# Block-causal attention into a gated MLP: how the row maxima reach the score products, and how the row sums are totalled

## The chip, the cores and the metric

The kernel runs on one core of a Trainium2 chip. The metric is the device time of one execution in microseconds. Five engines work side by side, each through its own list of instructions in order: TensorE (PE in the profile; its weight loads are shown as PEld), VectorE (DVE), ScalarE (ACT), GpSimd (POOL) and SyncE (SP), which here only issues DMA transfers. An instruction that waits for another engine holds up everything behind it in its own engine's list.

## The reference

```python
scores = scale * np.matmul(q, k.transpose(0, 1, 3, 2))     # 8 batches, 8 heads, 576 x 64
mask = block_i >= block_j                                   # blocks of 64
scores = np.where(mask, scores, -1000000000.0)
scores = scores - np.max(scores, axis=-1, keepdims=True)
attn = np.exp(scores)
attn = attn / (np.sum(attn, axis=-1, keepdims=True) + 1e-09)
x = np.matmul(attn, v)                                      # then heads side by side: 4608 x 512
a = x @ w1; b = x @ w2                                      # 512 x 1024 each
h = a * b @ w3                                              # 1024 x 1024
return h @ w_out                                            # 1024 x 512
```

## The kernel before, in words

The work goes by pairs of heads: 32 pairs (eight batches of four), and the two heads of a pair are `j = 0` and `j = 1`. For each head TensorE makes transposed scores (keys on the partitions, queries along the row) in tiles of 128 keys, `s_tile` (L255), ScalarE takes their exponential, and TensorE multiplies by the values (`pv`, L312). Numbers are kept as sums of a high and a low piece, so a product of two full numbers is two or three matmuls.

**The maxima.** A softmax row needs its maximum. `shift_mask` (L174) makes the scores once more, in 16 bits, as the products `mx` (L192, six tiles, up to 512 wide), VectorE reduces each to a column of the tile `m` (L196), TensorE turns the nine columns into nine rows (`mt`, L200), ScalarE copies these with a minus sign (`ms`, L202), and `shift` (L207) sends them by DMA into rows of the operand tiles `qk0` and `qk1` (L218): nine rows of 64 numbers for each head, laid out along one partition. There they stand as one more row of the contraction, so that the score product itself subtracts the maximum. For a pair `n` that is done while pair `n - 1` is at work. Up to pair 4 these transfers go on ScalarE's queue, from pair 5 on on SP's (`queue`, L168). The same queue of SP carries the load of the raw q, k and v of a pair (`load`, L101, 896 KB, two buffers), the copies of q and k to the other half of the partitions (L232, L233) and the outputs (L447).

**The second copy of the operands.** `prep_qk` (L220) casts q and k of a head into `qk0` or `qk1` on VectorE (L166), copies by DMA, and GpSimd makes the low piece (L235). `prep_v` (L238) casts the values on ScalarE and GpSimd makes their low piece `vs` (L248). The load of pair `n + 2` overwrites the buffer of pair `n`, so it waits for the last reader of that buffer, which is L248 for `j = 1`. That step in turn runs only when the value product of the pair ahead has let go of `vs`.

**The row sums.** `sums` (L330) reduces the sums over the keys to `part` on VectorE, `total` (L335) adds across partitions with one fp32 matmul of 36 columns against a 0/1 matrix (`groups4`, part of the tile `ident`), and `norm` takes the reciprocal and multiplies.

**The order.** TensorE's order is written out: for each pair and head a row of letters in `PLAN` (L46) is read from left to right. S is the next score tile or part of one, V and U the next value product, M the next step of `shift_mask` for the next pair, A and B steps of `prep_qk`, F the next piece of the MLP (six or so matmuls), R `sums`, N takes the values, Q prepares values and loads, T is `total` and the division. The MLP of a batch runs as F steps while the next batch's attention is at work; `DELAY` lets the first few F steps of pair 4 pass, which sets how far the MLP runs behind. The first four pairs have their own plan and share TensorE with the preparation of the weights. The other engines' lists are made by a scheduler from the program, so an instruction can stand there earlier or later than in the source.

## Time and profile before

| what | value |
|---|---|
| median of 3 timed runs | 971.45 us (969.41 to 972.49) |
| the profiled execution's own time | 970.15 us |
| span of its instructions | 968.3 us |
| PE busy | 938.8 us (97%) |
| DVE / ACT / POOL busy | 692.3 / 556.6 / 617.5 us |
| chain that ended last | PE 89% of the span |
| mean granted clock of TensorE | 0.996 |

In a row of a timeline stand the start in us from the span's start, the length in us, the engine, the line of the kernel, the operation, what it writes and reads, its shape and how many instructions were merged; in brackets the idle time ahead of it and who ended it. On SP a row is the issue of a transfer, not the transfer. Matmuls are pipelined, so their cost is read from start to start: one of 288 columns takes 0.13 us of TensorE, although each row says 0.29.

### The profile page before, as it was taken

The page shows a single profiled execution, that of the slowest core. Times are in us where ns is not written, and L with a number is a line of the kernel's source. Part 1 is how long each engine was busy: PE and PEld are TensorE (multiplying, and loading weights), DVE is VectorE, ACT ScalarE, POOL GpSimd, SP SyncE. Part 2 cuts the span into 40 slices and gives each one's busy share as a digit, 9 for nine tenths or more (in the row PEclk, how much of TensorE's full clock was granted, in tenths as well). Part 3 has the DMA queues.
Part 4 walks back from the last instruction along what each step waited for, and adds up shares of the span by engine and source line. Part 5 has one row for each costly group of instructions (what it writes and reads, how often), then busy time and mean ns, then how long its engine had stood idle before and what let it go on. Part 6 is the DMA issues. An engine that isn't in the chain of part 4 may idle for free.

```text
span 968.3 us, 18335 instructions
## 1 busy us (share of the span) xinstructions
PE 938.8 (97%) x6624; PEld 878.7 (91%) x6624; DVE 692.3 (72%) x1230; ACT 556.6 (57%) x1451; POOL 617.5 (64%) x605
## 2 busy tenths in 40 slices
PE   3898899999999999999999999999999999999998
PEld 1454469999999999999999999999999999999998
DVE  6787767788777777787787777777887777774100
ACT  7768736556565556565656555565555656553221
POOL 6766737677766767677776767676777667672211
PEclk9899999999999999999999999999999999999999
DMA  8976512212212221321222222222122122100000
GB/s 303 305 230 204 158 51 64 86 32 72 76 58 82 65 88 52 88 65 47 66 76 64 71 81 64 78 61 88 33 69 75 58 82 64 50 13 26 7 20 26
DMA packets 31303, 79.81 MB, mean 82 GB/s; under 512 B 5356, under 2 KB 13676, under 8 KB 31212
## 3 DMA queue, kind: packets, MB, share of 16 engines
q1 hardware_dynamic: 29788, 76.26, 25.7%
q10 hardware_dynamic: 1424, 2.38, 1.0%
q8 instruction: 52, 0.85, 0.4%
q14 instruction: 39, 0.32, 0.1%
HBM read 50.76 MB, written 9.44 MB: 62 GB/s over the span
## 4 chain that ended last, share of the span: by engine, by line
PE 89%; ACT 3%; DVE 3%; POOL 2%; issue 1%; DMA 1%; ACTq 0%; SPq 0%; DVEq 0%; POOLq 0%
PE ab L426 42%; PE o L442 21%; PE s L265 9%; PE x L320 9%; PE mx L192 4%; PE w L407 2%; POOL wbits L152 1%; ACT wbits L151 1%; ACT wy L150 1%; PE x L304 1%; DVE m L196 1%; ACT pe L273 1%; DMA qk<-ms 1%; DVE w L153 0%; PE tot L337 0%
## 5 line engine op out<-in xcount | busy, mean ns | idle before, releaser
L286 POOL TENSOR_TENSOR rsum<-rsum,p 128x448 f32<-128x448 f32 x224 | 185.8, 829 | 86.8 <-ACT p L280 78.3
L283 DVE TENSOR_TENSOR pl<-p,ph 128x448 fp32r<-128x448 f32 x168 | 149.4, 903 | 59.9 <-ACT ph L281 59.0
L435 POOL TENSOR_TENSOR gl<-g,gh 128x288 fp32r<-128x288 f32 x128 | 114.4, 894 | 121.9 <-ACT gh L434 121.9
L265 PE MATMUL s<-qk 128*128 128x288 f32 (+4 forms) x768 | 155.2, 311 | 6.1 <-ACT pe L273 3.6
L235 POOL TENSOR_TENSOR qk<-raw,qk 64x1152 fp32r<-64x1152 f32 x58 | 155.0, 2673 | 8.6 <-issue 5.6
L426 PE MATMUL ab<-xh,w2h 128*128 128x288 f32 x512 | 153.8, 300 | 0.0
L442 PE MATMUL o<-gh,wh 128*128 128x288 f32 x512 | 153.6, 300 | 0.0
L426 PE MATMUL ab<-xh,w1h 128*128 128x288 f32 x512 | 151.1, 295 | 0.0
L426 PE MATMUL ab<-xl,w2h 128*128 128x288 f32 x512 | 151.0, 295 | 0.0
L426 PE MATMUL ab<-xl,w1h 128*128 128x288 f32 x512 | 151.0, 295 | 0.0
L426 PE MATMUL ab<-xh,w1l 128*128 128x288 f32 x512 | 150.9, 295 | 0.0
L426 PE MATMUL ab<-xh,w2l 128*128 128x288 f32 x512 | 150.9, 295 | 0.0
L442 PE MATMUL o<-gh,wl 128*128 128x288 f32 x512 | 150.9, 295 | 0.0
L442 PE MATMUL o<-gl,wh 128*128 128x288 f32 x512 | 150.8, 295 | 0.0
L434 ACT CAST gh<-g 128x288 fp32r<-128x288 f32 x128 | 55.4, 433 | 143.1 <-DVE g L433 143.0
L265 PEld LDWEIGHTS s<-qk 128*128 128x128 f32 (+1 forms) x768 | 116.0, 182 | 17.9 <-ACT pe L273 9.4
L281 ACT ACTIVATE ph<-s 128x288 fp32r<-128x288 f32 x336 | 131.5, 393 | 0.0
L196 DVE TENSOR_REDUCE m<-mx 128x1 f32<-128x64 f32 (+3 forms) x320 | 128.4, 447 | 2.2 <-PE mx L192 0.2
L280 ACT ACTIVATE p<-s 128x448 f32<-128x448 f32 x224 | 85.4, 381 | 51.2 <-PE s L265 50.4
L283 DVE TENSOR_TENSOR pl<-rsum,ph 128x288 fp32r<-128x288 f32 x112 | 75.6, 676 | 49.6 <-ACT ph L281 45.6
L320 PE MATMUL x<-ph,vs 128*128 128x128 f32 x336 | 110.4, 329 | 0.0
L433 DVE TENSOR_TENSOR g<-ab,a 128x288 f32<-128x288 f32 x128 | 56.6, 442 | 69.8 <-PE ab L426 69.0
(76 smaller groups left out, 2180.4 us busy)
## 6 DMA issues: line engine op xcount, KB each, us to landing
raw<-in_qkv SPq DMA_DIRECT2D x31, 896.0 KB
qk<-qk SPq DMA_DIRECT2D x108, 144.0 KB
out_t<-o SPq DMA_DIRECT2D x64, 144.0 KB
wraw<-in_w3t SPq DMA_DIRECT2D x16, 512.0 KB
wraw<-in_w SPq DMA_DIRECT2D x16, 512.0 KB
wraw<-in_wout SPq DMA_DIRECT2D x8, 512.0 KB
qk<-qk ACTq DMA_DIRECT2D x16, 144.0 KB
qk<-ms SPq DMA_DIRECT2D x54, 2.2 KB
```

What stands on the lines that cost most here:

```text
L196: nc.vector.reduce_max(m[:, col : col + 1], sc, axis=AX.X)
L235: (nc.gpsimd if "late" in tl or n * j else nc.vector).tensor_tensor(out=qk[j][o, 2:4], in0=rqk[o], in1=qk[j][o, 0:2], op=ALU.subtract)
L265: nc.tensor.matmul(t[ks, at : at + q1 - q0], qk[j][:, k, kr], qk[j][:, q, q0:q1], start=(s == 0), stop=(s == 1))
L280: nc.scalar.activation(p32, t[ks, at : at + w], AF.Exp, scale=SCALE)
L281: nc.scalar.activation(ph[ks, o : o + w], t[ks, at : at + w], AF.Exp, scale=SCALE)
L283: nc.vector.tensor_tensor(out=low, in0=p32, in1=ph[ks, o : o + w], op=ALU.subtract)
L286: nc.gpsimd.tensor_tensor(out=r, in0=r, in1=p32, op=ALU.add)
L320: nc.tensor.matmul(xps[:, to : to + w], v[:, c, :], pr[:, a : a + w], start=(u < 2 and s == 0), stop=(u in (0, len(PV) - 1) and s == len(p ...
L426: nc.tensor.matmul(t[:, 0:HALF], l[:, c, fs], r, start=(c == 0 and s == 0), stop=(c == NC - 1 and s == 2))
L433: nc.vector.tensor_tensor(out=g32, in0=acc[1][:, 0:HALF], in1=a32, op=ALU.mult)
L435: nc.gpsimd.tensor_tensor(out=gl[:, f, :], in0=g32, in1=gh[:, f, :], op=ALU.subtract)
L442: nc.tensor.matmul(t[:, 0:HALF], l[:, f, es], r[:, f, :], start=(f == 0 and s == 0), stop=(f == NF - 1 and s == 2))
```

## The change

Five edits:

1. For every pair but the first, the maxima are no longer turned by TensorE and copied by ScalarE. VectorE turns the whole tile `m` (128 x 32) in blocks of 32 x 32 into `mr`. `m` is now one tile, cleared once. A head's nine rows of 64 then stand as two times nine rows of 32, so `shift` sends two transfers for each head where it sent one. The minus sign moves into the constants.
2. The last score tile of a head ends in two narrow products (64 keys by 64 queries). A step boundary is put between them, and the plan sets maximum products behind each of the two. The last of the maximum tiles of a pair comes later, behind the value products, and the reduction's end and the first `shift` come directly after it.
3. In the plan for `j = 1` one F stands between R and T now; in exchange one less follows T.
4. `total` splits the sums into three 16-bit pieces by four small VectorE instructions and adds three 16-bit matmuls of 36 columns; the 0/1 matrix is kept in 16 bits as well (`groups`).
5. `DELAY` is 4 where it was 3.

```diff
 PLAN = (
-    "B F B F S F S B F F S S F F F S M S M U M V F V V F V F R V M Q N",
-    "A S S A F F F S F M S F F F S S M A U M V V V F V F F V N Q F R T M F F",
+    "B F B F S F S B F F S S F F F S M S M S M U V F V V F V F R V M Q N",
+    "A S S A F F F S F S F F F S S M S M A U V V V F V F F V M M N Q F R F T F",
 )
-DELAY = 3
+DELAY = 4
...
+    m = cpool.tile([P, 32], F32, name="m")
+    nc.gpsimd.memset(m, 0.0)
...
         nc.vector.tensor_tensor(out=m[:, 8:9], in0=m[:, 8:9], in1=m[:, 9:10], op=ALU.max)
+        if n:
+            mr = work.tile([P, 32], F32, tag="mr", name=f"mr{n}")
+            nc.vector.transpose(mr, m)
+            ms_of[n] = mr
+            shift(n, 0)
+            yield
+            return
...
-        row = qk[j][x : x + 1, 0, :].rearrange("p (i r) -> p i r", r=BLK)
-        queue(n).dma_start(out=row.bitcast(F32), in_=ms_of[n][:, j * BLK : (j + 1) * BLK].bitcast(F32))
+        row = qk[j][x : x + 1, 0, :].rearrange("p (i h r) -> p i h r", h=2, r=32)
+        for h in range(2):
+            at = j * BLK + h * 32
+            queue(n).dma_start(out=row[:, :, h, :].bitcast(F32), in_=ms_of[n][at : at + NB, :])
...
             for s, (k, q) in enumerate(((1, 2), (3, 0))):
+                if s and c == 4 and n >= EARLY:
+                    yield
...
     def total(n, part, rr):
-        nc.tensor.matmul(tot[:, 0 : S // 16], groups4, part, start=True, stop=True)
+        parts = work.tile([P, 3, S // 16], BF16, tag="parts", name=f"parts{n}")
+        part = part.rearrange("p j b -> p (j b)")
+        for i in range(2):
+            nc.vector.tensor_copy(parts[:, i, :], part)
+            rest = part if i == 0 else parts[:, 2, :]
+            nc.vector.tensor_tensor(out=rest, in0=part, in1=parts[:, i, :], op=ALU.subtract)
+        for i in range(3):
+            nc.tensor.matmul(tot[:, 0 : S // 16], tl["groups"], parts[:, i, :], start=(i == 0), stop=(i == 2))
...
-    consts[0:NB, 1] = 1.0
+    consts[0:NB, 1] = -1.0
```

On SP's queue, at the end of pair 17, where the maxima of pair 18 (`ms18`) are sent and the load of pair 20 (`raw20`) is issued, this stood before:

```order
173 L218 DMA qk0_86<-ms18_6303 1x9x64
174 L447 DMA out_t<-o32_6312 128x288
175 L218 DMA qk1_87<-ms18_6303 1x9x64
176 L105 DMA raw20_6648<-in_qkv 128x1792
177 L447 DMA out_t<-o32_6354 128x288
```

And this stands there now (`mr18` are the turned maxima of pair 18):

```order
173 L106 DMA raw20_6729<-in_qkv 128x1792
174 L229 DMA qk0_86<-mr18_6341 1x9x32 x2
175 L467 DMA out_t<-o32_6394 128x288
176 L229 DMA qk1_87<-mr18_6341 1x9x32 x2
177 L467 DMA out_t<-o32_6444 128x288
```

The load of 896 KB has moved from behind the maxima to ahead of them. The same holds at the end of every pair from 4 to 28. The load itself still waits for the GpSimd step on `vs` (L248 before, L259 now) of pair 18.

On VectorE, at the end of pair 19, between the last score differences (`pl`, `ph`) and the value sum `x32`, this stood before:

```order
641 L166 CAST qk1_87<-raw20_6648 64x1152
642 L283 TENSOR_TENSOR pl_1112<-p19_1_6962,ph_1110 128x192
643 L283 TENSOR_TENSOR ph_1110<-p19_1_6967,ph_1110 64x64
644 L196 TENSOR_REDUCE m20_6819<-mx20_4_6972 128x1 x2
645 L196 TENSOR_REDUCE m20_6819<-mx20_5_6980 128x1 x2
646 L333 TENSOR_REDUCE part19_6701<-rsum_1111 128x18
647 L198 TENSOR_TENSOR m20_6819<-m20_6819 128x1
648 L352 TENSOR_TENSOR x32_19_6699<-x19_1_6873,xlow19_1_7016 64x576
```

And now (`parts19` are the three 16-bit pieces):

```order
729 L296 TENSOR_TENSOR ph_1108<-p19_1_7049,ph_1108 64x64
730 L198 TENSOR_REDUCE m_91<-mx20_4_7054 128x1 x2
731 L346 TENSOR_REDUCE part19_6782<-rsum_1109 128x18
732 L170 CAST qk1_87<-raw20_6729 64x1152
733 L353 CAST parts19_7124<-part19_6782 128x36
734 L355 TENSOR_TENSOR part19_6782<-part19_6782,parts19_7124 128x36
735 L353 CAST parts19_7124<-part19_6782 128x36
736 L355 TENSOR_TENSOR parts19_7124<-part19_6782,parts19_7124 128x36
737 L198 TENSOR_REDUCE m_91<-mx20_5_7093 128x1 x2
738 L200 TENSOR_TENSOR m_91<-m_91 128x1
739 L372 TENSOR_TENSOR x32_19_6780<-x19_1_6949,xlow19_1_7103 64x576
740 L203 STREAM_TRANSPOSE mr20_7099<-m_91 128x32
```

The cast of `qk1` for the next pair has moved from ahead of the last score differences to behind the row sums, the last maximum is taken behind the four small instructions, and the turn of the maxima stands behind the value sum.

More of the change, by code (lines that the diff above doesn't have):

```diff
@@ L129, in open_late @@
         tl["late"] = pool
+        tl["groups"] = pool.tile([P, P], BF16, name="groups")
+        nc.gpsimd.tensor_copy(tl["groups"], groups4)
         tl["ph"] = pool.tile([P, PW], F32R, name="ph")
@@ L181, in shift_mask @@
         yield
-        m = work.tile([P, 32], F32, tag="m", name=f"m{n}")
         groups = [((7, 0, 512),), ((8, 0, 512),), ((0, 0, 64), (6, 0, 448)), ((1, 0, 128), (5, 0, 384)),
@@ L201, in shift_mask @@
         ms = work.tile([64, P], F32R, tag="ms", name=f"ms{n}")[32 : 32 + NB]
-        nc.scalar.mul(out=ms, in_=mt[0:NB, 0:P], mul=-1.0)
+        nc.scalar.copy(ms, mt[0:NB, 0:P])
         ms_of[n] = ms
```

## The prediction

> **What bounds the kernel now.** I read the page first, then TensorE's waits, then the timelines of all queues around one pair's end, since every edit lies there.
>
> ```profile
> span 968.3 us, 18335 instructions
> PE 938.8 (97%) x6624; PEld 878.7 (91%) x6624; DVE 692.3 (72%) x1230; ACT 556.6 (57%) x1451; POOL 617.5 (64%) x605
> ```
>
> ```profile
> PE mx L192 <- ACT qd L166: 12.2, 3, 5.9
> PE s L265 <- DMA qk<-ms: 1.5, 2, 1.0
> ```
>
> TensorE sets the time. It has waited for the maxima's transfers 1.5 us in all, twice, so these transfers land in time for nearly every pair. The question is what each edit takes off TensorE's list, and whether anything now reaches it late. The end of pair 15 on TensorE (start, length, what):
>
> ```profile
> 454.42 0.19 PE L320 MATMUL x<-ph,vs 128*128 128x64 f32 x1
> ...
> 455.18 0.29 PE L442 MATMUL o<-gl,wh 128*128 128x288 f32 x1
> 455.31 0.30 PE L337 MATMUL tot<-part,ident 128*128 128x36 f32 x2
> 455.45 0.28 PE L200 MATMUL mt<-ident,m 128*9 128x128 f32 x1
> 455.48 0.38 PE L442 MATMUL o<-gh,wh 128*128 128x288 f32 x1
> 455.70 0.29 PE L442 MATMUL o<-gh,wl 128*128 128x288 f32 x1
> ...
> 458.75 0.43 PE L265 MATMUL s<-qk 128*128 128x288 f32 x2
> ```
>
> I call the start of the next pair's score products E: 458.75 here. SP's queue ahead of it:
>
> ```profile
> 456.08 0.78 SPq L218 DMA_DIRECT2D qk<-ms  x1
> 456.98 0.37 SPq L447 DMA_DIRECT2D out_t<-o  x1
> 457.45 0.78 SPq L218 DMA_DIRECT2D qk<-ms  x1
> 458.33 0.40 SPq L105 DMA_DIRECT2D raw<-in_qkv  x1
> ```
>
> The first head's maxima are issued 2.67 us ahead of E, the load only at E - 0.42. At the end of the next pair, where TensorE works on the MLP's first half instead of its second (the pairs alternate so), it is tighter:
>
> ```profile
> 483.39 1.63 SPq L218 DMA_DIRECT2D qk<-ms  x2
> 485.12 0.40 SPq L105 DMA_DIRECT2D raw<-in_qkv  x1
> ```
>
> ```profile
> 485.60 0.42 PE L265 MATMUL s<-qk 128*128 128x288 f32 x2
> ```
>
> Issue to use is 2.2 us here, with no wait recorded: a lone transfer of maxima needs at most 2.3 us.
>
> **The change part by part.**
>
> *The total and the turn.* From 455.31 to 455.70 TensorE spends 0.39 us on the total (two records), the turn and one product of 288 columns, which alone costs 0.13: so 0.26 us for the first two. For 16-bit products as narrow the nearest rows are the maximum products behind the last value product:
>
> ```profile
> 442.53 0.19 PE L320 MATMUL x<-ph,vs 128*128 128x64 f32 x1
> 442.56 0.39 PE L192 MATMUL mx<-kb,qd 128*128 128x64 bf16 x2
> 442.63 0.85 PE L265 MATMUL s<-qk 128*128 128x288 f32 x4
> ```
>
> They follow each other 0.03 us apart. Three of them, the last followed by a full-precision product at 0.11, make 0.17 instead of 0.26: -0.09 us a pair. At worst each takes 0.11, which is +0.07. For 27 pairs: -2.4 us, bounds -5 and +2.
>
> *Maximum products behind narrow ones.* The same products stand in other places; a narrow product gains or loses by what follows it (0.03 ahead of a 16-bit product, as above). Some gain, some lose; I take 0, bounds of 0.1 us a pair either way, 3 us.
>
> *The four small instructions.* The nearest rows for 128 x 36 are
>
> ```profile
> L339 DVE TENSOR_SCALAR rr<-tot 64x18 f32<-64x18 f32 x56 | 9.8, 175 | 1.0
> L355 DVE RECIPROCAL rr<-rr 128x18 f32<-128x18 f32 x32 | 8.4, 262 | 0.6
> ```
>
> so 0.2 us each, 0.8 together. The total's products now stand some 2.6 us ahead of E, one F (six products, 0.8 us) later than before; the pieces are ready about E - 3.7 by the chain below. No wait, with 1.1 us to spare; that F is the cover, and without it 0.3 would be left. `DELAY` gives the division back the step that the move took: nothing.
>
> *What reaches SP's queue, and when.* Here is the cost. The load now stands ahead of the maxima, and waits for GpSimd's step on `vs`. That step stands on GpSimd behind the low piece of `qk1`, which needs VectorE's cast of `qk1`, and that cast now stands behind the row sums. VectorE before:
>
> ```profile
> 448.62 0.74 DVE L196 TENSOR_REDUCE m<-mx 128x1 f32<-128x128 f32 x2
> ...
> 450.34 0.76 DVE L166 CAST qk<-raw 64x1152 fp32r<-64x1152 f32 x1 [0.57 <-PE s L265]
> ...
> 452.07 1.22 DVE L196 TENSOR_REDUCE m<-mx 128x1 f32<-128x192 f32 x4
> 453.20 0.77 DVE L333 TRANSPOSE_TENSOR_REDUCE part<-rsum 128x18 f32<-128x576 f32 x1
> ...
> 455.31 0.76 DVE L352 TENSOR_TENSOR x<-x,xlow 64x576 f32<-64x576 f32 x1 [0.59 <-ACT xlow L351]
> ```
>
> Before, the sums end at 453.97. Now the cast (0.76) and two of the four reductions (some 0.5) no longer stand ahead of them, the two of 448.62 (0.74) do, so they end near 453.45, E - 5.3. The cast follows, to E - 4.55. GpSimd before, at the two ends:
>
> ```profile
> 452.03 2.67 POOL L235 TENSOR_TENSOR qk<-raw,qk 64x1152 fp32r<-64x1152 f32 x1
> 455.89 0.88 POOL L248 TENSOR_TENSOR vs<-raw,vs 128x320 fp32r<-128x320 f32 x1 [1.19 <-ACT vs L166]
> ```
>
> ```profile
> 481.78 0.80 POOL L435 TENSOR_TENSOR gl<-g,gh 128x288 fp32r<-128x288 f32 x1 [0.23 <-ACT gh L434]
> 483.15 0.88 POOL L248 TENSOR_TENSOR vs<-raw,vs 128x320 fp32r<-128x320 f32 x1 [0.57 <-ACT vs L166]
> ```
>
> From E - 4.55: 2.67 for the low piece, to E - 1.9; at every other end 0.80 for `gl`, to E - 1.05; 0.88 for `vs`: E - 0.95 or E - 0.15. (Before it was E - 1.98 and E - 1.57.) SP waits there, and behind it on its queue wait both heads' maxima and the outputs. So the load is issued at E - 0.9 or E - 0.1. The maxima are by then turned: pieces to E - 3.75, two reductions 0.6, the maximum 0.3, the value sum 0.76, the turn 0.2 (bounds 0.18 and 0.78, by L339 and by the turn of 576 columns): E - 1.85, at the other ends some 0.5 later.
>
> Then the wire. Engines' busy shares by microsecond after the load issued at 458.33 (the last two columns are the DMA engines' share and GB/s):
>
> ```profile
> 460.00:461.00 1.00, 1.00 (x9) 1.00 (x8) 0.81 (x1) 0.95 (x3) 0.49 (x1) 1.00 0.83 337
> 461.00:462.00 1.00, 1.00 (x9) 0.99 (x8) 0.46 (x1) 0.20 (x2) 0.00 (x0) 1.00 1.01 395
> 462.00:463.00 1.00, 1.00 (x9) 0.99 (x8) 0.00 (x0) 1.00 (x3) 0.11 (x1) 1.00 0.59 218
> 463.00:464.00 1.00, 1.00 (x10) 1.00 (x9) 0.72 (x1) 0.91 (x3) 1.00 (x1) 1.00 0.00 0
> ```
>
> All sixteen engines carry it until about 4.3 us after its issue. The only row with maxima sent next to a load is from the early pairs, on ScalarE's queue, in the chain that ended last:
>
> ```profile
> 98.19 5.22 DMA qk<-ms
> ```
>
> 5.22 us instead of 2.3. So I let the maxima land when the load has passed: 4.3 us and, an estimate, 0.3 for the end of the transfer, or 4.6 after the load's issue: E + 3.7 and E + 4.5. The Trainium skill's "DMA: Bandwidth & Descriptors" (Queues, rings and completion order) says that on each DMA engine the descriptors of one issuing queue are taken in ring order; no run here shows a small transfer behind a load on SP's own queue. The score tile's first product needs no maxima, the second does. TensorE stands for 3.65 us at 12 ends and 4.4 us at 13 (pairs 4 to 28): 43.8 + 57.2 = 101.0 us. If VectorE had nothing else in the way, the sums could end 0.7 us earlier, which leaves 3.0 as the low bound, 75 us; 4.7 is the high one, 118. At the last two ends there is no load, and the second of two issues (0.78 apart) is late by itself: E - 1.85 + 0.8 + 2 is some 0.9 each, 1.9 together.
>
> *The clock.* A standstill of this length has a second price:
>
> ```profile
> 42.30:45.70 3.40, 1.41 (x4) 0.34 (x2) 2.85 (x3) 3.38 (x7) 2.64 (x5) 1.00 0.91 343
> 45.70:49.10 3.40, 3.32 (x8) 2.34 (x9) 2.39 (x4) 3.31 (x7) 2.16 (x2) 0.51 0.68 204
> ```
>
> ```profile
> 45.78 0.61 PE L192 MATMUL mx<-kb,qd 128*128 128x512 bf16 x1 [2.07 <-ACT qd L166]
> ```
>
> After 2.07 us of idle TensorE the granted clock (third figure from the end) was 0.51 for the next 3.4 us. At half the clock 3.4 us of work lose 1.7; part of the slow stretch falls into the standstill, so I take 1.2 at each of 25 ends: 30 us, bounds 0 and 43.
>
> *The first pairs.* Their maxima go on ScalarE's queue: eight issues more (0.78 each, by the row at 456.08), and ScalarE now waits for VectorE's turn where it made the rows itself; a step over TensorE is saved. I take +2, bounds -2 and +8.
>
> Sum on the profiled execution (970.15 us): -2.4 + 101.0 + 1.9 + 30 + 2 = +132.5, or 1102.7. The median of the timed runs is 1.3 above that execution: 1104.
>
> **The rivals.**
>
> A. The standstill comes, but the clock falls only after a whole window of 3.4 us (the length of the slow row) without work. A standstill of 3.65 or 4.4 us holds a whole window in (3.65 - 3.4) / 3.4 = 7% or (4.4 - 3.4) / 3.4 = 29% of cases: some 5 ends of 25, 6 us instead of 30, and 1080 in all. Against it: 2.07 us did it once. It is the rule of the Trainium skill's "TensorE: Matmul & The Clock Gate" (HAM oscillation): one idle window of some 3.4 us, and the rate is halved. Chance 0.27.
>
> B. The maxima are not held up by the load, and land 2.3 us after their own issue. Behind the load's issue (0.40) the second of two, 0.78 later, lands at E + 2.4 or E + 3.2, so 12 x 2.4 + 13 x 3.2 = 70 us, and 20 us for the clock: 1063. Against it stands the row of 5.22 us. Chance 0.13.
>
> C. The load gets away much earlier than by my chain, and only the maxima's own lateness is left: 0.75 to 1.1 us at 27 ends, 25 us, no clock: 996. It needs GpSimd's step on `vs` by E - 5.5, when the values it overwrites are still in use. Chance 0.05.
>
> D. Faster or no change: VectorE turns the maxima so early that both transfers land ahead of E, and the load waits behind or is away. It decides from the turn's end: at E - 3.1 or earlier nothing is late, and the 2.4 us of TensorE stay: 969. VectorE's list speaks against it, since the last maximum product alone ends near E - 4.1, with 1.9 us of work behind it. Chance 0.05.
>
> **How the numbers follow.** My forecast has 0.50, at 1104 us; its own range by the bounds is 1080 to 1130. About 0.3% (3 us) is what a measurement of this kernel can tell from no change. A, B and C are slower by more; D lies at the edge, 0.02 faster and 0.03 the same. Slower: 0.50 + 0.27 + 0.13 + 0.05 = 0.95. For 8 in 10 the range takes in my case, A with a shorter standstill, and part of B: 1045 to 1130; C and D are left out.
>
> **What would show it.** Right: in the waits TensorE's `s` products wait for the transfer of `mr` some 25 times, 3.5 to 4.5 us each, and on SP the load's row stands ahead of the maxima's, issued less than 1 us before E; the granted clock falls below 1 throughout the stages of attention; the total's products don't wait. Wrong: a load issued well ahead of E - 2 breaks the VectorE and GpSimd chain; maxima that land 2.3 us after a load's issue break the wire's part; a full clock breaks the 30 us. If TensorE never waits for the maxima, the whole cost is wrong.

## The result, and the profile after

The changed kernel takes 1165.26 us in the median (1162.33 to 1166.76, 6 runs); the kernel before took 971.09 (968.45 to 972.93, 6 runs) beside it. The ratio is 1.1998, with a 95% interval of 1.1973 to 1.2024: 194 us slower. The direction was forecast, the size was not: 1165 lies above the range of 1045 to 1130.

The head of the page of the changed kernel:

```profile
span 1160.5 us, 18675 instructions
PE 1000.5 (86%) x6621; PEld 913.5 (79%) x6621; DVE 824.0 (71%) x1373; ACT 548.5 (47%) x1420; POOL 611.8 (53%) x607
```

TensorE is no longer busy throughout: 160 us of the span are idle, where 29.5 were. VectorE is busy 132 us longer, far more than its new instructions should take: at the forecast 0.8 us for the pieces and 0.2 for the turn, 27 pairs make 27 us. What TensorE waits for (total us, times, longest):

```profile
PE ab L446 <- DVE g L453: 51.6, 28, 3.1
PE s L278 <- DMA qk<-mr: 47.2, 25, 3.3
PE tot L357 <- DVE parts L353: 22.1, 13, 1.8
```

The second row is the one that was forecast, at half its size. The first and the third were not forecast: products of the MLP's first half wait until VectorE has emptied their buffer by making `g`, and the total waits for its pieces. The rest is the clock:

```profile
core 0: 1160.5 us, clock 0.954
```

A clock of 0.954 costs 0.046 x 1160.5 = 53 us, where 0.996 cost 4. (That takes the slow time for work, which it nearly all is: behind 150 us TensorE stood idle in 3 of the 92 us of slow stretches.) So the 192 us of span are, roughly: mr 45.7 more than before, g 51.6, pieces 22.1, clock 49; the other 23 are smaller waits, the first pairs (3.6: pair 4 starts at 139.81, not 136.24) and what is left, which the waits don't show.

**Where VectorE's time went.** Its groups by shape (busy us, mean ns of one), of the changed kernel, and one group of the kernel before:

```profile
L355 DVE TENSOR_TENSOR part<-part,parts 128x36 f32<-128x36 f32 x28 | 67.5, 2412 | 1.0
L355 DVE TENSOR_TENSOR parts<-part,parts 128x36 bf16<-128x36 f32 x28 | 5.5, 196 | 1.0
L200 DVE TENSOR_TENSOR m<-m 128x1 f32<-128x1 f32 x32 | 5.8, 181 | 0.0
```

```profile
L198 DVE TENSOR_TENSOR m<-m 128x1 f32<-128x1 f32 x32 | 19.1, 595 | 0.0
```

Two subtractions of the same size, one behind the other, take 2412 and 196 ns. The timeline of VectorE and that of GpSimd, at the end of pair 15, say why:

```profile
537.68 0.76 DVE L170 CAST qk<-raw 64x1152 fp32r<-64x1152 f32 x1
538.47 0.18 DVE L353 CAST parts<-part 128x36 bf16<-128x36 f32 x1
538.69 2.61 DVE L355 TENSOR_TENSOR part<-part,parts 128x36 f32<-128x36 f32 x1
541.33 0.88 DVE L353 CAST parts<-part 128x36 bf16<-128x36 f32 x1
542.25 0.20 DVE L355 TENSOR_TENSOR parts<-part,parts 128x36 bf16<-128x36 f32 x1
...
543.80 0.21 DVE L203 STREAM_TRANSPOSE mr<-m 128x32 f32<-128x32 f32 x1
```

```profile
538.58 2.66 POOL L246 TENSOR_TENSOR qk<-raw,qk 64x1152 fp32r<-64x1152 f32 x1 [2.49 <-DVE qk L170]
541.32 0.86 POOL L259 TENSOR_TENSOR vs<-raw,vs 128x320 fp32r<-128x320 f32 x1
```

The cast of `qk1` ends at 538.44, GpSimd starts its low piece at 538.58, and the subtraction that VectorE starts at 538.69 ends at 541.30, 0.06 us behind GpSimd's instruction. The next cast ends 0.03 us behind GpSimd's next one. So a small instruction of VectorE stands for as long as GpSimd's lasts; in what follows I call that a hold. It was there to be seen before the change, on the maximum of one column (L198, 595 ns in the mean above, 181 ns now):

```profile
453.90 0.82 DVE L198 TENSOR_TENSOR m<-m 128x1 f32<-128x1 f32 x1
```

It ended at 454.72, and the low piece of the row quoted in the prediction (452.03, 2.67 us) at 454.70. There it cost nothing that the waits show.

TensorE at the same end, and at the end of the next pair, where it works on the MLP's first half:

```profile
542.26 0.41 PE L357 MATMUL tot<-parts,groups 128*128 128x36 bf16 x2 [1.75 <-DVE parts L353]
546.97 0.37 PE L278 MATMUL s<-qk 128*128 128x288 f32 x1 [1.69 <-DMA qk<-mr]
```

```profile
574.42 0.40 PE L446 MATMUL ab<-xh,w2h 128*128 128x288 f32 x1 [3.07 <-DVE g L453]
582.10 0.58 PE L278 MATMUL s<-qk 128*128 128x288 f32 x1 [2.41 <-DMA qk<-mr]
```

SP ahead of the first of these two, the load and then both transfers of the first head's maxima:

```profile
542.20 0.35 SPq L106 DMA_DIRECT2D raw<-in_qkv  x1
544.04 1.59 SPq L229 DMA_DIRECT2D qk<-mr  x2
```

In VectorE's list `g` stands behind the held subtraction, so TensorE waits 3.07 us for it. I call the stretch from a pair's last score product to E its tail. The forecast's chain can be laid beside the trace. These are times in us from the end of a pair's last score product, at the ends where TensorE works on the second half of the MLP (median over pairs 6 to 29, from starts and ends in the trace; the forecast's, given from E, with E at 8.45):

| | before | forecast | after | e1 | e20 | e14 |
|---|---|---|---|---|---|---|
| cast of qk1 ends | 0.79 | 3.90 | 3.90 | 3.90 | 0.79 | 0.79 |
| GpSimd's low piece ends | 4.39 | 6.55 | 6.70 | 6.72 | 4.41 | 4.39 |
| pieces ready | - | 4.70 | 7.90 | - | 5.13 | 5.18 |
| total starts on TensorE | 5.04 | 5.85 | 5.78 | 5.83 | 6.01 | 5.82 |
| vs done, load may go | 6.46 | 7.50 | 7.63 | 7.68 | 6.60 | 6.46 |
| maxima turned | - | 6.60 | 9.47 | 7.77 | 6.69 | 4.66 |
| E | 8.45 | 8.45 | 11.01 | 8.42 | 8.57 | 8.38 |

The columns e1, e20 and e14 are experiments below. At these ends the cast, the low piece and the load came within 0.15 us of the forecast, the pieces 3.2 us later, and the maxima were turned 2.9 us later. At the other ends, with the MLP's first half, the chain of the load did not hold: the cast comes at 4.55, the low piece at 7.31, and `vs` is done only at 10.73, where the forecast had 8.30. GpSimd makes a `gl` between the two (574.97, at the end of pair 16), and that waits for the `g` behind the held subtraction.

### The profile page after: what moved, and what is told of

It is laid out like the page before. It is cut to its first block, busy times and chain, and to the rows that moved or that the text cites. A ratio compares the mean times of both kernels' runs of the same rounds, so it can differ in the third digit from the quotient of the medians.

```text
span 1160.5 us, 18675 instructions
## 1 busy us (share of the span) xinstructions
PE 1000.5 (86%) x6621; PEld 913.5 (79%) x6621; DVE 824.0 (71%) x1373; ACT 548.5 (47%) x1420; POOL 611.8 (53%) x607
## 4 chain that ended last, share of the span: by engine, by line
PE 47%; DVE 28%; issue 9%; DMA 8%; ACT 6%; POOL 1%; SPq 0%; ACTq 0%; DVEq 0%; POOLq 0%
PE ab L446 24%; PE o L462 7%; DMA qk<-mr 6%; PE s L278 6%; DVE part L355 6%; PE w L427 3%; DVE m L198 3%; DVE pl L296 3%; PE x L333 3%; DVE x L372 2%; DVE qk L170 2%; PE mx L194 2%; DVE part L346 2%; DVE parts L353 2%; DVE g L453 2%
## 5 line engine op out<-in xcount | busy, mean ns | idle before, releaser
L296 DVE TENSOR_TENSOR pl<-p,ph 128x448 fp32r<-128x448 f32 x168 | 168.3, 1028 | 96.8 <-ACT ph L294 96.8
L455 POOL TENSOR_TENSOR gl<-g,gh 128x288 fp32r<-128x288 f32 x128 | 103.2, 806 | 220.8 <-ACT gh L454 220.8
L278 PE MATMUL s<-qk 128*128 128x288 f32 (+4 forms) x768 | 172.0, 324 | 53.2 <-DMA qk<-mr 47.2
L446 PE MATMUL ab<-xh,w2h 128*128 128x288 f32 x512 | 162.1, 317 | 51.6 <-DVE g L453 51.6
L296 DVE TENSOR_TENSOR pl<-rsum,ph 128x288 fp32r<-128x288 f32 x112 | 98.2, 878 | 101.5 <-ACT ph L294 101.5
L446 PE MATMUL ab<-xh,w1h 128*128 128x288 f32 x512 | 159.7, 312 | 3.1 <-ACT a L451 2.7
L462 PE MATMUL o<-gl,wh 128*128 128x288 f32 x512 | 157.4, 308 | 2.9 <-POOL gl L455 2.5
L446 PEld LDWEIGHTS ab<-xh,w2h 128*128 128x128 f32 x512 | 100.9, 197 | 60.2 <-DVE g L453 60.2
L198 DVE TENSOR_REDUCE m<-mx 128x1 f32<-128x64 f32 (+3 forms) x320 | 132.4, 445 | 1.9
L446 PEld LDWEIGHTS ab<-xh,w1h 128*128 128x128 f32 x512 | 102.7, 201 | 6.3 <-ACT a L451 5.9
L462 PEld LDWEIGHTS o<-gl,wh 128*128 128x128 f32 x512 | 101.1, 197 | 5.9 <-POOL gl L455 5.9
```

The source lines that it names most:

```text
L198: nc.vector.reduce_max(m[:, col : col + 1], sc, axis=AX.X)
L278: nc.tensor.matmul(t[ks, at : at + q1 - q0], qk[j][:, k, kr], qk[j][:, q, q0:q1], start=(s == 0), stop=(s == 1))
L296: nc.vector.tensor_tensor(out=low, in0=p32, in1=ph[ks, o : o + w], op=ALU.subtract)
L446: nc.tensor.matmul(t[:, 0:HALF], l[:, c, fs], r, start=(c == 0 and s == 0), stop=(c == NC - 1 and s == 2))
L455: nc.gpsimd.tensor_tensor(out=gl[:, f, :], in0=g32, in1=gh[:, f, :], op=ALU.subtract)
L462: nc.tensor.matmul(t[:, 0:HALF], l[:, f, es], r[:, f, :], start=(f == 0 and s == 0), stop=(f == NF - 1 and s == 2))
```

## The experiments

Each kernel is the changed one with the edit shown, unless it says "kernel before". Ratios are to the kernel before, run beside it, with 95% intervals; where ratios are taken from each other, a hundredth is 9.7 us.

### One part at a time

**e2: kernel before, with the new total alone** (edit 4).

> The kernel before with only the total changed to three 16-bit pieces and three products. T: on VectorE's list the pieces come here behind the maximum of m, which itself lasts until GpSimd's low piece of qk1 is over, so no subtraction is held: about 0.2 us each; the pieces are some 0.3 to 0.6 us late for the total's products, 27 times, so 5 to 20 us more than before: 975 to 990 us. R1 (the three pieces are slow wherever they stand): the first subtraction lasts 2.4 us here too, 1020 us or more. Third possibility, the pieces come in time: 968 to 971 us.

Measured: 981.90 us, 1.0105 (1.0075 to 1.0136), as theory T had it. TensorE waits 4.4 us for the pieces, 14 times.

**e3: kernel before, with VectorE's turn alone** (edit 1).

> The kernel before with only the turn of the maxima changed: VectorE turns them, two transfers for each head. T: on SP's queue the maxima stand ahead of the load here, and they are ready sooner than before; no wait for mr worth more than 2 us in all, TensorE loses the turn: 967 to 972 us. Rival R3 (two transfers of nine rows of 32 for each head are late by themselves, wherever they stand): waits for mr of 0.5 us or more at most ends, 980 us or more.

Measured: 972.92 us, 1.0004 (0.9986 to 1.0021): no change. The turn that leaves TensorE and two transfers for one together make no difference that can be measured.

**e8: both, with the old plan.**

```diff
-PLAN, DELAY and the boundary in the score tile as changed
+PLAN, DELAY = 3 and s_tile as before
```

> The changed kernel with the plan of before (edits 1 and 4 together: VectorE's turn and the total as three 16-bit products, nothing moved). The total alone on the old plan took 1.0105 times the kernel before, the turn alone 1.0004. Theory H: the cast of qk1 is back ahead of the row sums, GpSimd's low piece ends before or just as the pieces start, the maxima go ahead of the load: 975 to 990 us, ratio 1.003 to 1.02, hardly a wait for mr. Rival V: pieces and turn together make VectorE late, 1020 or more. Rival L agrees with H here.

Measured: 982.12 us, 1.0108 (1.0083 to 1.0133). Its one new wait:

```profile
PE tot L355 <- DVE parts L351: 4.7, 14, 0.4
```

At the 14 ends with a `g` in VectorE's tail the pieces come 0.4 us late. So edits 1 and 4 together cost 10 us, and the other 184 come when the plan is added to them.

**e7: kernel before, with the new plan alone** (edits 2, 3 and 5).

> The kernel before with the new plan alone (edits 2, 3 and 5: maximum products behind narrow ones, the MLP step ahead of the total, the extra step in the score tile), with TensorE's turn and the full-precision total of before. Theory H: the cast of qk1 stands behind the row sums as in the changed kernel, GpSimd's low piece starts with it and holds the maximum of m for 1.6 us, TensorE's turn waits for that, and the load stands ahead of the maxima on SP: 1110 to 1170 us, with some 20 waits or more of 3 to 5 us for the maxima's transfers. Rival V (the new instructions of VectorE, turn and pieces, make it late): 970 to 990. Rival L: 1045 to 1110 by the load alone, with the maximum of m no longer than before (0.6 us).

Measured: 1117.90 us, 1.1515 (1.1477 to 1.1554). There are no pieces here to be held; the hold falls on the maximum of one column, and TensorE's turn waits for that:

```profile
L198 DVE TENSOR_TENSOR m<-m 128x1 f32<-128x1 f32 x32 | 50.2, 1570 | 0.4
```

```profile
PE mt L200 <- DVE m L198: 73.9, 28, 3.1
```

The transfers were waited for only 17.9 us in all, 19 times, at most 2.9: less than expected, since TensorE already stands ahead of them. The plan by itself costs 147 us.

### The hold

**e1: the old total, no pieces.**

```diff
-        parts = ...; four VectorE instructions; three 16-bit matmuls
+        nc.tensor.matmul(tot[:, 0 : S // 16], groups4, part, start=True, stop=True)
```

> The changed kernel with the total as before: one fp32 matmul, no 16-bit pieces; all else as changed. Theory T (two separate costs: VectorE's first subtraction of the pieces waits 2.4 us for GpSimd's low piece of qk1 and makes TensorE wait for the gate product g, 51.6 us, and for the pieces, 22.1 us; and the load ahead of the maxima on SP's queue holds up the score products): both waits of 74 us vanish, the waits for mr stay and grow from 47 us toward the 101 us of the forecast, since nothing puts the score products off any more; 1060 to 1105 us. Rival R1 (the pieces cause everything, the load's place costs nothing by itself): waits for mr below 10 us, 965 to 985 us. Rival R2 (the load's place is the root, the pieces only follow it): 1150 us or more.

Measured: 1164.46 us, 1.1981 (1.1951 to 1.2010), as slow as with the pieces. Theory T of that text had the waits right (those for the pieces are gone, those for `g` are down to 8.7 us, those for mr have grown), but the time is 60 us above its range, where R2 had it. It is slow in another way:

```profile
PE s L278 <- DMA qk<-mr: 111.8, 27, 4.7
```

```profile
540.29 1.75 DVE L200 TENSOR_TENSOR m<-m 128x1 f32<-128x1 f32 x1
542.07 0.76 DVE L365 TENSOR_TENSOR x<-x,xlow 64x576 f32<-64x576 f32 x1
542.86 0.21 DVE L203 STREAM_TRANSPOSE mr<-m 128x32 f32<-128x32 f32 x1
```

The hold moves to the next instruction that can be held, the maximum, 1.75 us instead of 0.15. In this kernel TensorE does what was forecast for the change: it runs through its tail (E at 8.42) and then waits 4.1 us for the maxima, 27 times. At the last two ends, which have no load, it still waits 1.8 and 2.2 us, where 0.9 was forecast, because the maxima are late by themselves.

**e5: GpSimd's low piece of qk1 cut to 16 columns of each part.** The second head's scores lack their low part.

```diff
-tensor_tensor(out=qk[j][o, 2:4], in0=rqk[o], in1=qk[j][o, 0:2], ...)
+w = 16 if j and n > NPAIR else S
+tensor_tensor(out=qk[j][o, 2:4, 0:w], in0=rqk[o, :, 0:w], in1=qk[j][o, 0:2, 0:w], ...)
```

> The changed kernel, but GpSimd's low piece of qk1 (L246, 64x1152, 2.66 us) is made for 16 columns only from pair 5 on, so the scores of the second head lack their low part: work is left out. Theory H (GpSimd's low piece holds the first VectorE instruction with two operands that starts while it runs, 2.4 us an end; the plan of the change has put the cast that starts it into the tail): the subtraction of the pieces falls from 2412 ns to about 0.2 us, the waits of TensorE for g (51.6 us) and for the total's pieces (22.1 us) go nearly to nothing, the load gets away near E - 2.7 and the maxima behind it still land about 4.8 to 5.1 us after its issue, so the waits for mr stay at 45 to 65 us; with a better clock, 1030 to 1060 us. Rival L (the load ahead of the maxima is the whole cost, the long subtraction is only how the profile draws a wait): the waits for mr grow by what the others lose, and it stays at 1120 to 1165. Rival V (VectorE simply has too much to do in the tail, nobody holds it): the subtraction gets no shorter when GpSimd is idle, 1150 or more.

Measured: 1133.02 us, 1.1655 (1.1618 to 1.1692). The hold is gone, and with it the waits for the pieces:

```profile
L356 DVE TENSOR_TENSOR part<-part,parts 128x36 f32<-128x36 f32 x28 | 5.6, 199 | 1.0
```

```profile
PE s L279 <- DMA qk<-mr: 78.1, 27, 5.2
PE ab L447 <- DVE g L454: 18.4, 28, 0.7
```

That settles whose work held VectorE. But the time is in rival L's range, and as in its text the waits for mr grow by part of what the others lose: TensorE reaches E 2.7 us sooner, while the load gets away only 1.3 us sooner, so the wait behind the load grows from 47 to 78 us and the clock stays at 0.953. What one stall gives back, the next takes.

**e9: nothing left out; GpSimd issues the low piece of qk1 behind its low pieces of x.** The scheduler then also puts the maxima ahead of the load.

```diff
+        with tc.issue_after(tl["xl"]) if "xl" in tl and j and n > NPAIR else nullcontext():
             ... the low piece of qk[j]
```

> The changed kernel, whole, but GpSimd issues the low piece of qk1 behind its last low piece of x (an order on its own queue, no work left out), so it runs after E instead of in the tail; on SP the scheduler then puts the maxima ahead of the load. Theory H: no instruction of VectorE is held in the tail, the subtraction of the pieces lasts 0.2 us, the waits for g and for the pieces go, and only the lateness of the maxima by VectorE's own list is left, 0.3 to 1.2 us an end: 980 to 1010 us, clock over 0.99. Were the load alone the cost (rival L), about the same time, but the long subtraction would stay. Rival V: VectorE's list as such is too long: 1060 or more. A risk for every theory: the low piece now holds VectorE's first subtractions after E, which would show as waits of TensorE for pl.

Measured: 1068.04 us, 1.0997 (1.0972 to 1.1021). The subtraction is short (197 ns), the clock 0.994, and still 97 us are lost:

```profile
PE ab L447 <- DVE g L454: 33.0, 42, 1.2
PE s L279 <- DMA qk<-mr: 13.1, 27, 1.1
```

The risk named in the expectation came about: behind E the low piece (536.76, 2.78 us) meets one of VectorE's first subtractions of the new pair, of a shape that takes 0.44 to 0.57 us when free, and `g` comes behind it:

```profile
537.54 2.32 DVE L297 TENSOR_TENSOR pl<-rsum,ph 128x288 fp32r<-128x288 f32 x1 [0.54 <-ACT ph L295]
539.79 0.45 DVE L454 TENSOR_TENSOR g<-ab,a 128x288 f32<-128x288 f32 x1
```

TensorE waits for these subtractions 3.8 us in all, and 33.0 for `g`. The time is that of rival V; how much of it is the list's length and how much the hold behind E, this run alone doesn't say (e17 goes on from here).

### The load

**e4: no raw loads from pair 8 on**; the pairs work on old data.

```diff
-                            load(n + 2)
+                            raw_of[n + 2] = raw_of[n]      # from pair 8 on
```

> The changed kernel without the loads of raw q, k and v from pair 8 on: the pairs work on old data again, so the output is not the reference's. T: the waits for g and for the pieces (74 us) stay; the waits for mr fall from 47 us to some 30, because at every other end the maxima themselves are issued only 0.9 us ahead of the score products and the second of two transfers lands 1.7 us behind them, and at the others 0.6 us; 1140 to 1155 us. R2 (the load's place is the root of all): the waits for mr vanish and the others with them, below 1050 us. If only the load mattered for mr: waits for mr below 5 us, 1115 us.

Measured: 1120.00 us, 1.1525 (1.1489 to 1.1561). The waits for mr fall from 47.2 to 20.0 us, and the clock rises:

```profile
core 0: 1116.2 us, clock 0.976
```

The fall is at the ends of one kind only. Where TensorE works on the MLP's first half, the waits go from 31.4 to 4.8 us; where it works on the second, from 15.8 to 15.2. There the maxima, turned at 9.47, are late without any load. This is the end of pair 15, where the changed kernel waited 1.69 us:

```profile
526.03 0.40 PE L278 MATMUL s<-qk 128*128 128x288 f32 x1 [1.42 <-DMA qk<-mr]
```

The loads are worth 46 us of the 194 in the changed kernel, clock included, not 133.

### Inside the plan

**e10: without edit 2** (maximum products and score tile as before; the moved MLP step and DELAY 4 stay).

```diff
-    "A S S A F F F S F S F F F S S M S M A U V V V F V F F V M M N Q F R F T F",
+    "A S S A F F F S F M S F F F S S M A U M V V V F V F F V N Q F R F T M F",
...
-                if s and c == 4 and n >= EARLY:
-                    yield
```

> The changed kernel without edit 2: the maximum products, the row of the last maximum and the unsplit last score tile stand as before, edit 3 (one MLP step ahead of the total) and the rest stay. The order of VectorE has the cast of qk1 back behind the 128x320 subtraction, ahead of the row sums. Theory P (edit 2 alone puts the cast, and with it GpSimd's low piece, into the tail; all else follows from that): 972 to 985 us, the subtraction of the pieces near 0.2 us, the waits for the total's pieces gone (4.7 us with the old plan). Rival S (the moved step costs by itself, since the division and the low pieces of x come later): 1000 or more, with waits for x or for g.

Measured: 1001.22 us, 1.0310 (1.0284 to 1.0337). The waits for the pieces are gone as expected, but the time is that of rival S, with the wait for `g` that it named:

```profile
PE ab L444 <- DVE g L451: 18.4, 14, 1.3
```

**e11: without edit 3** (the step behind the total again, DELAY 3).

```diff
-    "... V M M N Q F R F T F",
+    "... V M M N Q F R T F F",
```

> The changed kernel without edit 3: the MLP step stands behind the total again, DELAY is 3. Theory P: the cast stays behind the row sums, so the held subtraction (2.4 us), the waits for g and for mr stay, and the total's products, 0.8 us earlier on TensorE, wait longer for their pieces: 1150 to 1190 us. Rival S (a good part of the 194 us is the moved step): 1080 or less.

Measured: 1128.52 us, 1.1624 (1.1580 to 1.1668), faster than the change. TensorE waits 70 us for the pieces, but only 7.5 for `g` and 1.5 for mr. Two things were taken back here, and the second is what counts: e15 below has the step and DELAY 3, and its ratio is 1.1645, not to be told from this one. So neither range of the expectation holds, and the moved step by itself makes no difference that can be told here.

**e12: the second head's maximum products where they stood** (first head as changed, DELAY 4).

```diff
+    "A S S A F F F S F M S F F F S S S M A U M V V V F V F F V M N Q F R F T F",
```

> The changed kernel with the second head's maximum products back where they stood before (M behind the fourth score step and behind U), the split last score product kept without a maximum in the split; first head and the rest as changed. The order has the cast of qk1 ahead of the 128x192 subtraction and of the row sums, and the maxima ahead of the load. Theory P: 970 to 985 us, no long subtraction, no wait for mr. Rival S: 1000 or more.

Measured: 1058.85 us, 1.0903 (1.0874 to 1.0931), far above theory P's range. The hold is on the maximum (1500 ns), `g` is waited for 39.6 us.

**e13: only the last maximum product back.**

```diff
+    "A S S A F F F S F S F F F S S M S M A U M V V V F V F F V M N Q F R F T F",
```

> The changed kernel with only the last maximum product (mx5) back behind the first U, mx3 and mx4 left behind the later score steps. The order still has the cast of qk1 behind the row sums, but VectorE's turn ahead of it, and the maxima ahead of the load. Theory P: the hold is there (subtraction 2.4 us), the waits for g (3 us at every other end) and for the pieces (1.7 us at the others) stay, the waits for mr go: 1050 to 1110 us. If the load and the late maxima were what costs: 975 to 1000. If only the late last maximum did harm: 975 to 1000 as well, with a short subtraction.

Measured: 1117.29 us, 1.1505 (1.1475 to 1.1535), 7 us above theory P's range, with the waits that it named: none for mr, the subtraction held (2496 ns), `g` 48.4 us and the pieces 22.6. So most of the 194 us are lost even where the maxima go ahead of the load and come in time.

### The phase of the MLP

e10 against e8 pointed to edit 5, which I had costed at nothing. The next four change `DELAY` alone.

```diff
-DELAY = 4
+DELAY = 3
```

**e14: e10 with DELAY 3**, that is edits 1, 3 and 4.

> The kernel without edit 2 (1001 us), but DELAY back at 3: the MLP step still stands ahead of the total, only the phase of the MLP's steps against the attention is as before. Theory D (DELAY 4 shifts the MLP by one step of 0.8 us against the attention, so that at every other end TensorE needs a product g while VectorE is busy with, or held in, its tail): the 18.4 us of waits for g go, the total's pieces are in time too, 970 to 978 us. Rival: the number does nothing, 1001.

Measured: 971.38 us, 0.9999 (0.9989 to 1.0010): no change. TensorE is where it was:

```profile
PE 937.0 (97%) x6621; PEld 873.7 (90%) x6621; DVE 731.3 (76%) x1373; ACT 545.4 (56%) x1420; POOL 621.0 (64%) x607
```

Neither `g` nor the pieces nor mr are waited for. One number made 30 us in e10. With DELAY 4 the MLP runs one step of 0.8 us behind, and TensorE wants the buffer that `g` must empty just while VectorE is in its tail.

**e15: the changed kernel with DELAY 3.**

> The changed kernel with DELAY 3 instead of 4 and nothing else. Theory D: the waits for g fall from 51.6 to some 7 us (that of the kernel with edit 3 undone, which has DELAY 3 as well); the hold of the pieces stays and now meets the total at all 27 ends instead of 13, 1.7 us each, 45 us; the maxima still go behind the load: 1090 to 1135 us. Rival: g is late wherever it stands, 1150 to 1170.

Measured: 1134.19 us, 1.1645 (1.1605 to 1.1685). In its trace, of an execution of 1142.38 us, `g` is waited for 9.4 us, the pieces 49.2, at ends of both kinds, and mr 35.4.

**e16: e12 with DELAY 3.**

> The kernel with the second head's maximum products back (1059 us), with DELAY 3. Theory D: its waits for g (39.6 us at 28 places, every other pair) go, the waits for the pieces (10 us at 13 ends) stay or spread to all ends (20 us): 980 to 1005 us. Rival: the split score product or the first head's plan costs by itself, 1030 or more.

Measured: 1084.69 us, 1.1168 (1.1147 to 1.1188): slower than e12, so the rival of that text holds, and DELAY 3 is not better everywhere. Against e14 only the first head's plan differs in TensorE's order. There too the cast (of qk0, 493.86) falls behind the row sums, so GpSimd's piece of it comes late (494.70 to 497.38), and `vs`, `gl` and a sum follow it without a gap, to 500.50. The last two run beside a subtraction of the second head, which starts at 498.72 and ends at 500.98. In the groups by shape:

```profile
L296 DVE TENSOR_TENSOR pl<-p,ph 128x448 fp32r<-128x448 f32 x56 | 115.3, 2059 | 31.4 <-ACT ph L294 31.4
```

They took 1243 ns before (L283 of the kernel before). TensorE waits 28.7 us for `g`, 25.9 for reductions of maxima and 15.4 for `gl`.

**e17: e9 with DELAY 3.**

> The kernel with GpSimd's low piece of qk1 behind that of x (1068 us), with DELAY 3. Theory D: its waits for g (33.0 us at 42 places) go, those for mr (13 us) stay: 1010 to 1040 us. Rival: 1060 or more.

Measured: 1046.89 us, 1.0776 (1.0757 to 1.0796). `g` falls to 6.5 us, so most of e9's wait for it came with the phase; but 24.7 us of waits for GpSimd's `gl` come instead, at 13 places in mid-pair. That `gl` stands behind the first head's low piece and `vs` (536.27 to 539.97), not behind the moved one. e11, e15 and e16, which have the changed plan of the first head and DELAY 3 too, wait 15 to 16 us for it at 13 places; e14, with the old plan of the first head, doesn't wait for it.

### One step

**e20: in each head one M step goes from between the two narrow score products to behind them.** Nothing else; DELAY is 4.

```diff
-    "... S M S M S M U V F V V F V F R V M Q N",
+    "... S M S S M M U V F V V F V F R V M Q N",
-    "... F F F S S M S M A U V V V F V F F V M M N Q F R F T F",
+    "... F F F S S S M M A U V V V F V F F V M M N Q F R F T F",
```

VectorE's list then has the cast ahead of the 128x192 subtraction again, as before the change.

> The changed kernel with one maximum product of each head moved one place: behind the second product of the last score tile instead of between its two products. VectorE's order then has both casts of qk ahead of the row sums again; on SP the load still stands ahead of the maxima, DELAY is 4. Theory C (the product in the split frees qk one product later, and for that the scheduler puts the cast behind the row sums; GpSimd's low piece then runs over the tail): the subtraction of the pieces falls from 2.4 us to 0.2 to 0.8, the waits for the pieces go and those for g fall below 20 us, while the load ahead of the maxima keeps TensorE waiting for mr 2.5 to 3 us an end, 70 to 85 us: about what the kernel without the low piece took, 1110 to 1140 us. Rival: the place of one product in the order does nothing to the hold, 1150 or more, with the subtraction at 2.4 us.

Measured: 1118.75 us, 1.1534 (1.1509 to 1.1559). The subtraction is at 196 ns, the pieces are in time, and the load is what is left:

```profile
PE s L278 <- DMA qk<-mr: 75.1, 27, 3.4
PE ab L446 <- DVE g L453: 16.5, 14, 1.3
```

So one M step of some 0.2 us on TensorE, moved by one place in each head, made the hold. (The 0.2 is a difference: from its first to its last score product the second head takes 7.41 us here and 7.64 in the kernel before, where that step stands among them.) The likely way, by the order of the two lists: while the step stands between the two score products, `qk` is free for the next cast one step later, and the scheduler puts the row sums ahead of the cast. Which of the two heads' steps matters more was not tried.

**e22: e20, with DELAY 3 and the load issued behind the first head's maxima.** Edits 1 to 4 are in it, edit 2 as in e20.

```diff
+                            with tc.issue_after(ms_of["dma"]) if n > EARLY else nullcontext():
                                 load(n + 2)
```

> That kernel, and besides SP issues the load behind the first head's maxima (an order on its queue, no work left out), and DELAY is 3. So all four edits are in it, with the cast early, the load behind and the phase of before. Theory C with what the load and DELAY have shown: no hold, no wait for g, and only the maxima's own lateness left, 0.4 to 0.8 us an end: 985 to 1010 us, clock over 0.99. If it comes out at 968 to 975, edit 2's later last maximum costs nothing by itself; at 1040 or more there is a cause that none of these runs has shown.

Measured: 1036.57 us, 1.0697 (1.0669 to 1.0725), above the 985 to 1010 expected. The subtraction is at 197 ns, no wait for `g` is left, the clock is 0.995, and yet 67 us are lost:

```profile
PE ab L446 <- ACT a L451: 25.6, 25, 1.4
PE s L278 <- DMA qk<-mr: 22.0, 27, 1.3
```

The maxima are late by themselves: turned at 6.68 us, sent some 0.1 later, the second of the two transfers 0.8 behind the first. That is edit 2's late last maximum. The other row is of my own making. The order on SP took the load one pair back, since the scheduler had issued it a pair ahead of its place in the program, and ScalarE's cast of the keys now waits for it, with the copy of `a` behind it in its list:

```profile
550.67 0.67 ACT L170 CAST kb<-raw 128x576 bf16<-128x576 f32 x1 [1.82 <-DMA raw<-in_qkv]
...
552.74 0.42 ACT L451 COPY a<-ab 128x288 f32<-128x288 f32 x1
```

```profile
553.22 0.40 PE L446 MATMUL ab<-xh,w1h 128*128 128x288 f32 x1 [1.31 <-ACT a L451]
```

What the kernel would take with the load in neither of the two places was not tried.

## Why the prediction was wrong, point by point

- **Direction: right. The load's chain: right at every other end.** "[T]hat cast now stands behind the row sums", and behind it the low piece, `vs` and the load: each within 0.15 us where TensorE works on the MLP's second half, 2.4 us too late for `vs` where it works on the first, by a wait for `g` that the forecast did not have.
- **The time from the load to TensorE: 4.6 us put, 4.77 at the end of pair 15 (542.20 to 546.97) and 5.16 at the next (576.94 to 582.10).** The first of these is luck. By e4 the maxima, late by themselves, would have come 0.3 us sooner there without any load. At the second the load does decide, as it does in e1 and e20, where TensorE goes on some 5 us after the load's issue.
- **The failing step: "0.2 us each, 0.8 together. [...] No wait, with 1.1 us to spare."** The four instructions took (21.1 + 67.5 + 5.5) / 28 = 3.4 us an end, and TensorE waited 22.1 us for the pieces and 51.6 for the `g` behind them, where the sum has nothing. I had taken their price from L339 and L355, instructions of another kind, which were not held where they ran beside GpSimd (456.10, beside the `vs` of 455.89), and had moved GpSimd's 2.67 us beside them without asking whether the two engines can run side by side. The rows that answered it were on hand: four reductions of 1.22 us that ran through beside GpSimd's piece (452.07), and, behind the row sums, the maximum of one column that ended with it (453.90). e5, e9 and e20 take the low piece away from the subtraction in three ways, and each time it lasts 196 to 199 ns. Leaving the pieces out does not bring the forecast's time, though: in e1 the hold falls on the maximum and the time stays.
- **"`DELAY` gives the division back the step that the move took: nothing."** It cost 30 us without the hold (e10 against e14) and 34 with it (the change against e15). It shifts all of the MLP by a step against the attention, not only the division. Which value is better depends on the rest: with e12's plan DELAY 3 costs 26 us more (e16). With DELAY 3 the moved step is even good: it is the cover that the pieces need (e8 against e14, 10 us), as the prediction said of that F.
- **The maxima behind the load: right in size where no other stall of TensorE comes first.** 102.9 us forecast with the last two ends, 111.8 in e1. In the changed kernel TensorE stands 1.75 or 3.07 us earlier in the same tail, the maxima gain on it, and 47.2 are left. Of these 20.0 stay when there are no loads (e4): the maxima are turned 2.9 us later than I had put.
- **The clock: 30 us forecast, 49 more than before.** I let part of the slow stretch fall into the standstill. e1 shows the term by itself: 27 standstills of 4.1 us, and a clock of 0.949 loses 59 us, 4 of them as before, which leaves 2.0 each where I took 1.2. In its trace only 11.6 of the 107 us of slow stretches behind 150 us are idle. Rival A's rule, a whole empty window of 3.4 us, is refuted for this kernel by waits of 2.7 to 3.4 us that cost a slow stretch each in e20 (last section).
- **"Some gain, some lose; I take 0."** What it is on TensorE itself, no run separates. But the step between the two score products decides where the cast stands: 1.1998 against 1.1534, 45 us.
- **The total and the turn on TensorE, -2.4 us: not seen in the time.** e14 has both and is at 0.9999, give or take 1 us. Its TensorE is busy 1.8 us less (937.0 against 938.8), so part of it may be there and be lost elsewhere.
- **First pairs +2: 3.6.**

So the mechanism that I had was there, but in the changed kernel its waits come to 45.7 us where I put 102.9. A hold between two engines and one number of the plan make 73.7 more where I put nothing, and the clock takes 49 instead of 30. The two stalls lie in the same microseconds, which is why the parts don't add up: the hold away 33 us (e5), the load away 46 (e4), DELAY 34 (e15), one step 45 (e20), edit 2 with DELAY all 194 (e14). Either stall alone makes most of the loss: 1119 us without the long hold (e20), 1117 without any wait for the maxima (e13). No version that ran is faster than the kernel before; e3 and e14 are as fast.

## What to carry to other kernels

Where a change moves a long GpSimd instruction, look which VectorE instructions will run beside it, and find in the trace of before one of the same kind that already does: compare its length with the length of its like elsewhere. In a list that a scheduler makes, ask of each moved instruction what it frees, since a step of 0.2 us can turn two long instructions round. And when several stalls stand in one tail, price the tail as a chain from a common start, not as a sum: the first stall hides the next, and taking one away shows the one behind it.

## What the runs showed of the hardware

**Which instructions are held.** Beside a GpSimd subtraction, VectorE's instructions with two inputs in SBUF (the on-chip memory in which the kernel's tiles stand) were held, whatever their size (128x1: 1.75 us in e1; 128x36: 2.61; 128x288: 2.32 in e9), and so were some 128x36 casts, which have one input (0.88 us beside L259). Reductions were not: neither those of the maxima, which read the products where TensorE writes them (the four of 452.07), nor those of the row sums, which read SBUF (453.20, 0.77 us). The Trainium skill's "SBUF — State Buffer" (Who interferes with whom) says that a VectorE instruction with two inputs there contends with a GpSimd instruction that reads there, and that the one issued first blocks the other for its whole length; the trace agrees, with 26 of 28 subtractions that end some 0.05 us behind GpSimd's. That a port is what they share, no run here shows.

**The clock.** Counted in the clock records of the traces behind 150 us, slow stretches of 3.4 us against the waits of TensorE there:

| kernel | waits over 1.25 us | slow stretches | clock |
|---|---|---|---|
| e10 | 14 of 1.3 | 0 | 0.993 |
| e12 | 14 of 2.2 | 7 | 0.984 |
| e4 | 15 of 3.1, 22 of 1.4 to 1.8 | 14 | 0.976 |
| e20 | 25 of 2.7 to 3.4, one of 1.25 | 25 | 0.954 |
| e1 | 25 of 3.9 to 4.7, 2 of 2 | 31 | 0.949 |

```profile
core 0: 1055.9 us, clock 0.984
```

The row is that of e12. The Trainium skill's "TensorE: Matmul & The Clock Gate" (HAM oscillation) names gaps of over some 3.4 us as what brings the half rate; the traces here differ: 2.2 us did it every second time, and 3 us nearly always. Waits of up to 1.4 us brought none (e10, e22).

**A wait seems to cost more than its length.** e22 has about the clock of e14 (0.995 and 0.992), stands idle 49 us longer (79.9 against 30.9) and takes 66 us longer. The other 17 us, over its 52 waits for `a` and for the maxima, are 0.3 us each. This is an estimate: the order of the maximum products differs too, and its share is not known. The matmuls overlap (0.13 us from start to start, 0.29 long) and each wait ends the overlap once, which would make 0.16 of it.
